# Attention into a gated feed-forward layer on one core: the second batch's keys in three full chunks and a shared half, the weights' high parts on GpSimd, and the second product in groups of units

## The chip, the cores and the metric

The kernel runs on one core of one Trainium2 chip. The metric is the device time of one execution in microseconds (us), median of three runs. The core has a TensorE (PE; its weight loads are shown apart as PEld), a VectorE (DVE), a ScalarE (ACT), a GpSimd (POOL) and a SyncE (SP), which issues most of the DMA transfers.

## The reference

```python
# q, k, v: (4, 12, 448, 64); cap = 30
scores = cap * tanh((q @ k.T / sqrt(64)) / cap)
attn = exp(scores - max) / (sum + 1e-9)
x = (attn @ v)  reshaped to (1792, 768)
out = (sigmoid(x @ w_gate) * (x @ w_val)) @ w_out      # 768 -> 1536 -> 768
```

## The kernel before

The 12 heads of each of the 4 batches are taken two at a time: 24 pairs of heads, numbered n = 0 to 23, six for each batch. A pair holds 448 queries and 448 keys. Its steps are the transposes of keys and queries (`emit_T`), the scores with keys on the partitions (`emit_S`, one chunk of keys m at a time, tanh on ACT), the exponentials (`emit_exp`, ACT), the product with the values (`emit_PV`; the values carry 64 columns of ones, so that the sums of the exponentials come out beside it), the reciprocal of the sums and the scaling (`emit_rd`, `emit_out`). The row x of a batch, split into a high and a low fp32r part (`xspl`), then goes through the feed-forward layer, `moe(b)`. Every large product is made of three fp32r products: high by low, high by high, low by high.

`moe(b)` eats 36 units of weights. The first 24 are columns of w_gate and w_val in turn (a unit is 18 matmuls on tile `h`); the other 12 are pieces of w_out for the product on the tiles `o`: two halves t of 384 columns, each with six units of `KU` = 2 chunks of the inner dimension, and for each unit six matmuls for each of three chunks of rows (five in the last batch). One `o` tile is kept for each chunk of rows during a half, and a half's units come one after the other.

In batch 0 each unit is made from 64-bit input: `convert_w` has one ACT step (L739) and three DVE steps (L740 to L742), and `split_w` makes the high part (`o.hi`, L207 on ACT; on POOL for the first four units) and the low part (`o.lo`, L213 on DVE). Four buffers `wspl` (`WB`) hold split units, and two hold raw ones (`pair`). The split units are stored in device memory, and later batches load them (`load_to`, `wspl<-wd`, 768 KB each) when a buffer comes free. The first four units (`KEEP`) are stored through ACT's queue when PE takes them.

The attention of batch 0 runs by itself at the start. That of batch b + 1 runs between the pieces of `moe(b)`: both are generators, and each `yield` tells how much PE work was emitted; the loop at the kernel's end takes from the one that is behind its share. `o.head` is the attention's expected amount for a head. PE and ACT run in the order in which the code is written; the order on DVE, POOL and SP is a scheduler's.

Three kinds of pairs exist. Pairs 0 to 5 (`alone`) and 6 to 11 multiply exponentials and values in plain fp32 (`direct`); the others split the exponentials. Pairs 0 to 5 are `packed`: three chunks of 128 keys, and the last 64 keys of both heads side by side in one chunk, whose scores are three matmuls over all 128 rows and whose values (`emit_R`) are two matmuls of 64 rows, one for each head. Pairs 6 to 11 are `even`: four chunks of 112 keys for each head. Tiles in PSUM come from `two_banks` (two buffers of two banks), `ps_v` (one bank) and `ps_m` (three banks, for `h`, `o` and some `pv`).

Of the kernel before, what the change touches and what calls it, by code (L numbers as in the profile page):

```python
# [9 lines left out]
F32 = mybir.dt.float32  # L10
# [9 lines left out]
P = 128  # L20
# [78 lines left out]
def _load_inside(engines, t, src, n, runs=False):  # L99

    s = _pair(src, n)
    order = "(p c) d -> p c d" if runs else "(c p) d -> p c d"
    for h in range(2):
        engines[h % len(engines)].dma_start(
            out=t[0:src.shape[2] // NCH, :, h, :], in_=s[h].rearrange(order, c=NCH)
        )


def _load_evenly(nc, t, src, n):

    s = _pair(src, n)
    for h in range(2):
        nc.sync.dma_start(
            out=t[0:src.shape[2] // NCH, h * NCH:(h + 1) * NCH],
            in_=s[h].rearrange("(p c) d -> p c d", c=NCH),
        )
# [63 lines left out]
class _Ops:  # L180
# [37 lines left out]
    def load_qk(self, n, evenly=False, packed=False):  # L218
# [4 lines left out]
        if packed:  # L223
            _load_k_packed(self.nc, [self.nc.sync], qk[:, 1], self.k, n)
        elif evenly:
            _load_inside([self.nc.sync], qk[:, 1], self.k, n, runs=True)
        else:
            _load_k(self.nc, qk[:, 1], self.k, n)
# [20 lines left out]
def _bounded_attention(o, x_done):  # L249
# [32 lines left out]
    packed = alone  # L282
# [5 lines left out]
    def even(n):  # L288

        return direct(n) and not packed(n)  # L290

# [4 lines left out]
    o.head = lambda b: 25 if direct(b * o.NPAIR) else 17.8 if b == B - 1 else 18.5  # L296
# [19 lines left out]
    def load_v(n):  # L316
# [8 lines left out]
        if packed(n):  # L325
            _load_v_packed(nc, s[:, :, 0:D], o.v, n)
        else:
            _load_evenly(nc, s[:, :, 0:D], o.v, n)
# [11 lines left out]
    def emit_T(n):  # L340
# [5 lines left out]
        if even(n):  # L346
            o.transpose_evenly(ps[:, 0, :], t[:, 1])
        else:
            for m in range(NC):
                nc.tensor.transpose(  # L350
                    ps[:, 0, m * P:(m + 1) * P], t[:, 1, m].rearrange("p h d -> p (h d)"), ident
                )
        o.transpose_evenly(ps[:, 1, :], t[:, 0])
        T[n] = ap.tile([P, 2, 2, BANK], F32R, tag="T", bufs=1, name=f"T{n}")
        w = S if even(n) else BANK
        hi, lo = T[n][:, 0, :, 0:w], T[n][:, 1, :, 0:w]
        if even(n):
            parts = [(hi, lo, ps[:, :, 0:w])]
        else:
            parts = [tuple(  # L360
                x.rearrange("p i s -> p (i s)")[:, 0:BANK + S] for x in (hi, lo, ps)
            )]
        for a, b, x in parts:
            o.hi("a", a, x)
            with o.tc.high_priority(offset=2 * AHEAD_OF):
                o.lo("v", b, x, a)

    def emit_S(n, m):
# [3 lines left out]
        w = QC if even(n) else P  # L372
        kh, kl = (T[n][:, i, 0, m * w:(m + 1) * w] for i in range(2))
# [3 lines left out]
        if packed(n) and m == NF:  # L377
            for i, (a, r) in enumerate(ops):
                nc.tensor.matmul(
                    ps[:, 0, 0:S], a, r, start=(i == 0), stop=(i == len(ops) - 1)  # L380
                )
            nc.scalar.activation(
                Pt[n][:, 0, NF, :], ps[:, 0, 0:S], AF.Tanh, scale=c["scale"]
            )
            return 4
        for i, (a, r) in enumerate(ops):
            for j in range(2):
                rows = half(j)
                nc.tensor.matmul(  # L389
                    ps[0:w, j, 0:S], a[rows], r[rows], start=(i == 0), stop=(i == len(ops) - 1)  # L390
                )
        nc.scalar.activation(  # L392
            Pt[n][0:w, :, m, :], ps[0:w, :, 0:S], AF.Tanh, scale=c["scale"][0:w]
        )
        return 4

    def emit_exp(n, j):
        rows = slice(0, QC if even(n) else P)
        t = Pt[n][rows, j, 0:NF if packed(n) and j == 1 else NC]
        nc.scalar.activation(t, t, AF.Exp, scale=c["cap"][rows])  # L400
# [20 lines left out]

    def new_pv(n, j):
        if alone(n) and not (j == 1 and n % 2 == 0):
# [14 lines left out]
    def emit_PV(n, j):  # L438
# [9 lines left out]
        if direct(n):  # L448
            for m in range(NC):
                nc.tensor.matmul(  # L450
                    pv, vs[n][0:QC, j * NC + m, :], Pt[n][0:QC, j, m, :], start=(m == 0),
                    stop=(m == NC - 1),
                )
                if m % 2 == 1:
                    yield 7.4
        else:
            (ph, pl), v = Phl.pop((n, j)), vs[n][:, j]
            for m in range(NF):
                nc.tensor.matmul(pv, v[:, m, :], pl[:, m, :], start=(m == 0), stop=False)  # L459
                nc.tensor.matmul(pv, v[:, m, :], ph[:, m, :], start=False, stop=False)  # L460
            nc.tensor.matmul(pv, v[:, NF, :], ph[:, NF, :], start=False, stop=True)  # L461
            yield 7
# [55 lines left out]
    qks[1] = o.load_qk(1, direct(1), packed(1))  # L518
    load_v(0)
    qks[2] = o.load_qk(2, direct(2), packed(2))  # L520
# [5 lines left out]
    for n in range(NP + 1):  # L526
        live, last = n < NP, n == o.NPAIR
        if live:
            due = emit_S(n, 0) + emit_S(n, 1)
            if n in PLAN:  # L530
# [519 lines left out]
```

## Time and profile before

| | |
|---|---|
| median of 3 runs | 758.19 us (757.61 to 758.44) |
| profiled execution | 757.79 us, its span 756.0 us |
| PE busy in the span | 742.5 us |
| DVE, ACT, POOL busy | 503.5, 379.4, 215.8 us |
| mean granted TensorE clock | 0.998 of full speed |

The span runs from the first to the last instruction; the rest of the time lies around it. PE's busy time counts overlapping matmuls once, so a matmul's own duration is longer than the step from one to the next. Stages in the span: batch 0's attention to about 75 us, batch 0's `h` units to 208.7, its `o` units to 264.8, and the same for the batches after it.

### The profile page before, as it was taken

The numbers are of one execution on the slowest core, as the hardware profiler recorded it, in microseconds if no ns is written. First come the engines' busy times: TensorE is split into PE (matmuls) and PEld (weight loads), VectorE is DVE, ScalarE is ACT, GpSimd is POOL, SyncE is SP. The second block draws the span as 40 slices with busy tenths as digits, with TensorE's granted clock in tenths as the row PEclk, the third lists the DMA queues.
The fourth block names the chain that finished last, engine by engine and source line by source line (L and its number), as shares of the span: only waits on it lengthen the run. The fifth ranks groups of instructions, "written<-read, shape, count | busy, mean of one in ns | idle before, by whom it ended". The sixth has DMA issues, their size and how long they took to land.

```text
span 756.0 us, 10362 instructions
## 1 busy us (share of the span) xinstructions
PE 742.5 (98%) x3922; PEld 642.4 (85%) x3922; DVE 503.5 (67%) x539; ACT 379.4 (50%) x419; POOL 215.8 (29%) x223
## 2 busy tenths in 40 slices
PE   8999999999999999999999999999999999999997
PEld 7555878788788888888899988888989999999996
DVE  2698788978989948988896638899877132322000
ACT  5888567767667456756574146655651011111000
POOL 1354010021210516464555305455452000000000
PEclk9999999999999999999999999999999999999999
DMA  4767898988899864444567954533369945463551
GB/s 100 214 160 164 277 335 262 302 283 263 257 268 379 264 250 127 136 152 139 165 175 241 307 165 134 145 107 123 126 176 328 321 155 182 154 195 98 180 164 57
DMA packets 133511, 151.78 MB, mean 201 GB/s; under 512 B 86860, under 2 KB 111948, under 8 KB 133452
## 3 DMA queue, kind: packets, MB, share of 16 engines
q1 hardware_dynamic: 131788, 147.56, 62.9%
q10 hardware_dynamic: 1664, 3.46, 1.3%
q8 instruction: 33, 0.54, 0.3%
q14 instruction: 26, 0.21, 0.1%
HBM read 118.75 MB, written 31.46 MB: 199 GB/s over the span
## 4 chain that ended last, share of the span: by engine, by line
PE 85%; DVE 6%; DMA 3%; ACT 2%; POOL 2%; issue 1%; SPq 0%; POOLq 0%; DVEq 0%; ACTq 0%
PE h L863 43%; PE o L954 22%; PE sc L389 6%; PE pv L450 4%; DMA wd<-wspl 2%; PE pv L460 2%; PE pv L459 2%; DVE rd L506 2%; PE tp L242 1%; PE pv L441 1%; PE tp L350 1%; DVE pair L742 1%; PE pv L461 1%; DMA v<-in_v_dram 1%; PE dn L498 1%
## 5 line engine op out<-in xcount | busy, mean ns | idle before, releaser
L863 PE MATMUL h<-xspl,wspl 128*128 128x448 f32 x1728 | 377.2, 372 | 0.1
L863 PEld LDWEIGHTS h<-xspl,wspl 128*128 128x128 f32 x1728 | 321.3, 188 | 41.9 <-issue 14.8
L954 PE MATMUL o<-wspl,gspl 128*128 128x384 f32 x864 | 159.5, 338 | 1.2 <-DVE gate L907 1.2
L954 PEld LDWEIGHTS o<-wspl,gspl 128*128 128x128 f32 x864 | 150.4, 188 | 6.0 <-issue 3.8
L205 POOL TENSOR_SCALAR gspl<-gate 128x448 fp32r<-128x448 f32 x48 | 41.3, 860 | 239.4 <-DVE gate L907 239.4
L392 ACT ACTIVATE t<-sc,scale 128x896 f32<-128x896 f32 (+1 forms) x90 | 85.9, 1003 | 33.1 <-PE sc L389 32.8
L207 ACT ACTIVATE wspl<-pair 128x768 fp32r<-128x768 f32 x68 | 57.4, 845 | 88.8 <-PE h L863 75.1
L907 DVE SCALAR_TENSOR_TENSOR gate<-gate,h 128x448 f32<-128x448 f32 x48 | 29.6, 616 | 83.6 <-PE h L863 69.1
L400 ACT ACTIVATE t<-t,capv 128x1792 f32<-128x1792 f32 (+2 forms) x48 | 83.2, 1738 | 0.1
L213 DVE TENSOR_TENSOR wspl<-pair,wspl 128x768 fp32r<-128x768 f32 x68 | 75.3, 1108 | 4.0 <-ACT wspl L207 3.9
L506 DVE RECIPROCAL rd<-rd 128x448 f32<-128x448 f32 x24 | 70.7, 2946 | 5.8 <-ACT rd L479 3.1
L904 ACT ACTIVATE gate<-h 128x448 f32<-128x448 f32 x48 | 26.0, 542 | 92.4 <-PE h L863 87.9
L389 PE MATMUL sc<-T 64*128 64x448 f32 (+1 forms) x540 | 69.1, 383 | 1.9 <-DVE T L213 1.7
L389 PEld LDWEIGHTS sc<-T 64*128 64x128 f32 (+1 forms) x540 | 46.4, 181 | 22.4 <-issue 11.2
L412 POOL TENSOR_TENSOR a<-t 128x448 f32<-128x448 f32 x24 | 31.4, 1309 | 76.6 <-ACT t L400 42.6
L976 DVE TENSOR_SCALAR osb<-o 128x384 f32<-128x384 f32 x22 | 11.9, 556 | 61.9 <-PE o L954 61.8
L207 ACT ACTIVATE ph<-t 128x1792 fp32r<-128x1792 f32 x24 | 40.7, 1698 | 14.8 <-PE pv L461 14.7
L213 DVE TENSOR_TENSOR pl<-t,ph 128x1344 fp32r<-128x1344 f32 x24 | 47.2, 1967 | 0.4
L213 DVE TENSOR_TENSOR gspl<-gate,gspl 128x448 fp32r<-128x448 f32 x48 | 38.1, 794 | 7.2 <-POOL gspl L205 6.9
L213 DVE TENSOR_TENSOR T<-tp,T 128x960 fp32r<-128x960 f32 (+1 forms) x24 | 27.3, 1135 | 22.8 <-ACT T L207 22.7
L742 DVE SCALAR_TENSOR_TENSOR pair<-w,pair 128x768 uint16<-128x768 uint32 x36 | 41.8, 1164 | 0.3
L739 ACT ACTIVATE pair<-w 128x768 f32<-128x768 f32 x36 | 32.5, 905 | 17.4 <-DVE wspl L213 12.3
(81 smaller groups left out, 735.0 us busy)
## 6 DMA issues: line engine op xcount, KB each, us to landing
wspl<-wd SPq DMA_DIRECT2D x72, 768.0 KB, 5.0
wd<-wspl SPq DMA_DIRECT2D x20, 768.0 KB, 5.5
pair<-wr SPq DMA_DIRECT2D x36, 384.0 KB, 3.1
w<-in_moe_w_gate_dram SPq DMA_DIRECT2D x12, 768.0 KB, 6.9
w<-in_moe_w_val_dram SPq DMA_DIRECT2D x12, 768.0 KB, 6.5
w<-in_moe_w_out_dram SPq DMA_DIRECT2D x12, 768.0 KB, 6.5
qk<-in_q_dram SPq DMA_DIRECT2D x46, 112.0 KB, 3.3
wr<-pair SPq DMA_DIRECT2D x12, 384.0 KB, 5.4
```

Of the source, the lines that this page charges most:

```text
L205: self.nc.gpsimd.tensor_scalar(dst, src, 1.0, 1.0, ALU.mult, ALU.mult)
L207: self.nc.scalar.activation(dst, src, AF.Copy)
L213: e.tensor_sub(dst, src, hi.bitcast(F32))
L389: nc.tensor.matmul(ps[0:w, j, 0:S], a[rows], r[rows], start=(i == 0), stop=(i == len(ops) - 1))
L392: nc.scalar.activation(Pt[n][0:w, :, m, :], ps[0:w, :, 0:S], AF.Tanh, scale=c["scale"][0:w])
L400: nc.scalar.activation(t, t, AF.Exp, scale=c["cap"][rows])
L412: nc.gpsimd.tensor_add(a, t[:, 0, :], t[:, 1, :])
L506: nc.vector.reciprocal(rd, rd)
L739: nc.scalar.activation(x, top.bitcast(F32), AF.Copy, scale=2.0 ** -112)
L742: nc.vector.scalar_tensor_tensor(half, low.bitcast(U32), 2.0 ** -29, half, ALU.mult, ALU.add)
L863: nc.tensor.matmul(ps, a, r, start=(kk == 0 and i == 0), stop=(kk == KD - 1 and i == 2))
L954: nc.tensor.matmul(ps, a, r, start=(y + kk == 0 and i == 0), stop=(y + kk == KF - 1 and i == 2),)
```

## The change

Pairs 6 to 11 become `packed` too. For them (`together`) the loop has a branch of its own, in which the values of both heads are multiplied in one run, into two banks of one `two_banks` tile, and the last chunk's scores go to `ps_v`. All 36 units of batch 0 have their high part made by POOL. In the second product the first two units of a half, and the last two, are taken as a group: all their matmuls for a chunk of rows before the next chunk. Units 0 to 2 are stored during the last pairs of batch 0 instead of when PE takes them. `o.head` for batch 1 goes from 25 to 23.5.

```diff
-    packed = alone
+    packed = direct
+    def together(n):
+        return direct(n) and not alone(n)
...
-    o.head = lambda b: 25 if direct(b * o.NPAIR) else 17.8 if b == B - 1 else 18.5
+    o.head = lambda b: 23.5 if direct(b * o.NPAIR) else 17.8 if b == B - 1 else 18.5
...
+        if packed(n) and m == NF:
+            if together(n) and n > o.NPAIR:
+                ps = o.ps_v.tile([P, S], F32, tag="v", name=f"sc{n}_{m}")
+            else:
+                ps = o.two_banks(f"sc{n}_{m}")[:, 0, 0:S]
...
     def new_pv(n, j):
-        if alone(n) and not (j == 1 and n % 2 == 0):
+        if together(n):
+            if j == 0:
+                two[n] = o.two_banks(f"pv{n}")
+            pv = two[n][:, j, 0:S] if j == 0 else two.pop(n)[:, j, 0:S]
+        elif alone(n) and not (j == 1 and n % 2 == 0):
...
+        if n > 0 and together(n - 1):
+            emit_R(n - 1)
+            emit_S(n, 0)
+            yield 5
+            for j in range(2):
+                for _ in emit_PV(n - 1, j):
+                    yield 6
+            for j in range(2):
+                emit_rd(n - 1, j)
+            emit_out(n - 1)
+            vs.pop(n - 1)
+            load_v(n + 1)
+            yield 8
+            emit_S(n, 1)
+            emit_S(n, 2)
+            if not packed(n):
+                yield 8
+            emit_S(n, NF)
+            yield 8
+            emit_T(n + 1)
+            qks[n + 2] = o.load_qk(n + 2, packed(n + 2))
+            yield 5
...
+            emit_exp(n, 0)
+            if not direct(n):
+                emit_P(n, 0)
+            emit_exp(n, 1)
+            split_v(n + 1)
...
+            if NC <= n <= o.NPAIR:
+                o.store_early(n - NC)
...
-        o.hi("p" if u < o.early else "a", s[:, 0, :], t)
+        o.hi("p" if u < NU else "a", s[:, 0, :], t)
...
-                for y in range(x, KF if x >= by_chunk else x + KU, KU):
-                    units.append((y, next_w(u)))
+                if x >= by_chunk:
+                    to = KF
+                elif x == 0 or not end and x == KF - 2 * KU:
+                    to = x + 2 * KU
+                else:
+                    to = x + KU
+                for y in range(x, to, KU):
+                    units.append((y, next_w(u) if y == x or end else w_spl.pop(u)))
...
+                if to > x + KU and not end:
+                    prepare_w(u - 1)
```

On PE, in the middle of `moe(0)`'s first product, the values of pair 7 (`pv`) and the first scores of pair 8 (`sc`) stood like this before:

```order
L389 MATMUL sc_0_1071<-T_982 112x448 x6
L389 MATMUL sc_1_1079<-T_982 112x448 x6
L863 MATMUL h_1_3_1048<-xspl_4_655,wspl_902 128x448 x3
L863 MATMUL h_1_3_1048<-xspl_5_697,wspl_902 128x448 x3
L863 MATMUL h_0_4_1106<-xspl_0_319,wspl_955 128x448 x3
L863 MATMUL h_0_4_1106<-xspl_1_405,wspl_955 128x448 x3
L450 MATMUL pv_0_1113<-t_834,vo_829 128x448 x2
L863 MATMUL h_0_4_1106<-xspl_2_491,wspl_955 128x448 x3
L863 MATMUL h_0_4_1106<-xspl_3_573,wspl_955 128x448 x3
L863 MATMUL h_0_4_1106<-xspl_4_655,wspl_955 128x448 x3
L863 MATMUL h_0_4_1106<-xspl_5_697,wspl_955 128x448 x3
L450 MATMUL pv_0_1113<-t_834,vo_829 128x448 x2
```

The same place of the changed kernel, one pair later (values of pair 8, first scores of pair 9):

```order
L413 MATMUL pv_1318<-t_1088,vo_935 128x448 x2
L365 MATMUL sc_0_1322<-T_1245 128x448 x6
L874 MATMUL h_0_6_1305<-xspl_4_667,wspl_1147 128x448 x3
L874 MATMUL h_0_6_1305<-xspl_5_712,wspl_1147 128x448 x3
L874 MATMUL h_1_6_1350<-xspl_0_319,wspl_1193 128x448 x3
L874 MATMUL h_1_6_1350<-xspl_1_405,wspl_1193 128x448 x3
L420 MATMUL pv_1318<-t_1088,vo_935 128x448 x3
L874 MATMUL h_1_6_1350<-xspl_2_491,wspl_1193 128x448 x3
L874 MATMUL h_1_6_1350<-xspl_3_579,wspl_1193 128x448 x3
L874 MATMUL h_1_6_1350<-xspl_4_667,wspl_1193 128x448 x3
L420 MATMUL pv_1318<-t_1088,vo_935 128x448 x3
L874 MATMUL h_1_6_1350<-xspl_5_712,wspl_1193 128x448 x3
```

A pair's values go from four groups of two matmuls to two matmuls of 64 rows and two groups of three, and half of the first scores comes later.

On PE, in `moe(0)`'s second product, the last two units of the first half (`wspl_1911`, `wspl_1963`) and the start of the second half before:

```order
L954 MATMUL o_0_0_1856<-wspl_1911,gspl_733 128x384 x6
L450 MATMUL pv_0_2066<-t_1772,vo_1767 128x448 x2
L954 MATMUL o_0_1_1857<-wspl_1911,gspl_733 128x384 x6
L954 MATMUL o_0_2_1858<-wspl_1911,gspl_733 128x384 x6
L954 MATMUL o_0_0_1856<-wspl_1963,gspl_733 128x384 x6
L450 MATMUL pv_0_2066<-t_1772,vo_1767 128x448 x2
L954 MATMUL o_0_1_1857<-wspl_1963,gspl_733 128x384 x6
L954 MATMUL o_0_2_1858<-wspl_1963,gspl_733 128x384 x6
```

The same two units (`wspl_1971`, `wspl_1982`) in the changed kernel:

```order
L970 MATMUL o_0_0_1877<-wspl_1971,gspl_751 128x384 x6
L970 MATMUL o_0_0_1877<-wspl_1982,gspl_751 128x384 x6
L420 MATMUL pv_2039<-t_1786,vo_1639 128x448 x3
L970 MATMUL o_0_1_1878<-wspl_1971,gspl_751 128x384 x6
L970 MATMUL o_0_1_1878<-wspl_1982,gspl_751 128x384 x6
L420 MATMUL pv_2039<-t_1786,vo_1639 128x448 x3
L970 MATMUL o_0_2_1879<-wspl_1971,gspl_751 128x384 x6
L970 MATMUL o_0_2_1879<-wspl_1982,gspl_751 128x384 x6
```

The second unit of a group is now wanted six matmuls after the first instead of eighteen, and both buffers come free at the group's end.

On POOL, at the same stage, the changed kernel's queue (with the tiles' numbers: `wspl27` is unit 27, `vs12` the split values of pair 12, `xspl1_4` part 4 of batch 1's row):

```order
L195 TENSOR_SCALAR vs12_2001<-v12_1853 128x8x64
L195 TENSOR_SCALAR wspl27_1886<-pair0_66 128x768
L195 TENSOR_SCALAR gspl0_751<-gate0_11_1766 128x448
L195 TENSOR_SCALAR xspl1_4_1872<-xraw1_929 128x448
L195 TENSOR_SCALAR wspl28_1971<-pair0_66 128x768
L195 TENSOR_SCALAR wspl29_1982<-pair0_66 128x768
L195 TENSOR_SCALAR wspl30_2016<-pair0_66 128x768
L195 TENSOR_SCALAR wspl31_2057<-pair0_66 128x768
L195 TENSOR_SCALAR vs13_2344<-v13_2114 128x8x64
L195 TENSOR_SCALAR wspl32_2122<-pair0_66 128x768
L195 TENSOR_SCALAR xspl1_5_2111<-xraw1_929 128x448
L195 TENSOR_SCALAR wspl33_2143<-pair0_66 128x768
```

Before, none of the `wspl` rows stood there; the sums of pair 12's exponentials (`a12`), which follow the last unit now, stood between `xspl1_4` and `vs13`.

## Rows read from the trace of the kernel before

**Rows 1.** The page, part 1: busy us, share of the span, instructions.

```profile
PE 742.5 (98%) x3922; PEld 642.4 (85%) x3922; DVE 503.5 (67%) x539; ACT 379.4 (50%) x419; POOL 215.8 (29%) x223
```

**Rows 2.** Windows: length, busy PE, PEld, DVE, ACT, POOL, clock, DMA share, GB/s.

```profile
75.00:209.00 134.00, 133.27 (x649) 106.19 (x647) 113.76 (x135) 91.07 (x110) 19.00 (x20) 1.00 0.88 281
209.00:265.00 56.00, 54.95 (x305) 47.51 (x304) 51.81 (x58) 35.11 (x39) 14.95 (x11) 1.00 0.91 306
...
556.00:599.00 43.00, 41.78 (x235) 40.75 (x234) 25.07 (x28) 8.61 (x9) 11.06 (x11) 1.00 0.96 297
```

**Rows 3.** The chain that ended last, from 104 us: start, us, what (records).

```profile
118.51 1.50 PE pv L450 x4
120.01 2.45 PE h L863 x12
...
127.01 1.42 PE sc L389 x12
```

**Rows 4.** The same chain, batch 0's attention.

```profile
66.87 0.75 PE pv L434 x4
67.62 4.71 PE pv L441 x12
```

**Rows 5.** Waits from 75 to 265 us: engine, line, waited for, us, times, longest.

```profile
ACT wspl L207 <- DMA wd<-wspl: 4.7, 2, 2.8
```

**Rows 6.** Timeline of PE at batch 2's second product; in brackets the idle time before.

```profile
557.67 2.36 PE L954 MATMUL o<-wspl,gspl 128*128 128x384 f32 x12 [1.22 <-DVE gate L907]
```

**Rows 7.** Timeline of DVE in batch 0's second product.

```profile
205.62 0.93 DVE L740 TENSOR_SCALAR pair<-pair 128x768 int32<-128x768 int32 x1
...
217.26 0.56 DVE L740 TENSOR_SCALAR pair<-pair 128x768 int32<-128x768 int32 x1 [0.98 <-ACT pair L739]
...
218.73 0.95 DVE L213 TENSOR_TENSOR wspl<-pair,wspl 128x768 fp32r<-128x768 f32 x1
...
242.60 0.56 DVE L740 TENSOR_SCALAR pair<-pair 128x768 int32<-128x768 int32 x1 [1.22 <-ACT pair L739]
...
251.06 2.50 DVE L213 TENSOR_TENSOR pl<-t,ph 128x1344 fp32r<-128x1344 f32 x1
...
254.54 1.81 DVE L213 TENSOR_TENSOR wspl<-pair,wspl 128x768 fp32r<-128x768 f32 x1
...
256.88 2.94 DVE L506 RECIPROCAL rd<-rd 128x448 f32<-128x448 f32 x1
...
262.70 1.56 DVE L213 TENSOR_TENSOR xspl<-xraw,xspl 128x448 fp32r<-128x448 f32 x1 [0.46 <-POOL xspl L205]
```

**Rows 8.** Timeline of PE in the same stage.

```profile
208.71 1.21 PE L954 MATMUL o<-wspl,gspl 128*128 128x384 f32 x6
...
250.25 13.02 PE L954 MATMUL o<-wspl,gspl 128*128 128x384 f32 x72
263.20 1.49 PE L389 MATMUL sc<-T 64*128 64x448 f32 x12
```

**Rows 9.** POOL's wspl group by form, then timelines of POOL and DVE around 205 us.

```profile
L205 POOL TENSOR_SCALAR wspl<-pair 128x768 fp32r<-128x768 f32 x4 | 3.3, 832 | 4.0 <-DVE pair L742 4.0
...
204.47 3.38 POOL L205 TENSOR_SCALAR xspl<-xraw 128x448 fp32r<-128x448 f32 x4 [2.79 <-ACT gate L904]
211.68 2.16 POOL L205 TENSOR_SCALAR gspl<-gate 128x448 fp32r<-128x448 f32 x1 [3.83 <-DVE gate L907]
...
206.47 0.96 DVE L213 TENSOR_TENSOR xspl<-xraw,xspl 128x448 fp32r<-128x448 f32 x1
...
208.58 0.61 DVE L213 TENSOR_TENSOR xspl<-xraw,xspl 128x448 fp32r<-128x448 f32 x1
...
212.44 0.98 DVE L741 SCALAR_TENSOR_TENSOR pair<-w,pair 128x768 int32<-128x768 int32 x1
```

**Rows 10.** DMA issues from 556 to 599 us (count, KB, us to landing); PE there.

```profile
wspl<-wd SPq DMA_DIRECT2D x12, 768.0 KB, 6.2
...
581.68 17.02 PE L954 MATMUL o<-wspl,gspl 128*128 128x384 f32 x96
```

More of the change, by code (lines that the diff above doesn't have):

```diff
@@ L96, in _pair, with _load_inside @@
     return src[b, 2 * p:2 * p + 2]
-def _load_inside(engines, t, src, n, runs=False):
+def _load_inside(engines, t, src, n):
     s = _pair(src, n)
-    order = "(p c) d -> p c d" if runs else "(c p) d -> p c d"
     for h in range(2):
         engines[h % len(engines)].dma_start(
[L105 to L115, printed above, removed]
+            out=t[0:src.shape[2] // NCH, :, h, :],
+            in_=s[h].rearrange("(c p) d -> p c d", c=NCH),
         )
@@ L324, in load_v @@
         nc.gpsimd.memset(s[:, :, D:], 1.0)
[L325 to L328, printed above, removed]
+        _load_v_packed(nc, s[:, :, 0:D], o.v, n)
         vs[n] = s
@@ L345, in emit_T @@
         ps = o.two_banks(f"tp{n}")
[L346 to L352, printed above, removed]
+        for m in range(NC):
+            nc.tensor.transpose(
+                ps[:, 0, m * P:(m + 1) * P], t[:, 1, m].rearrange("p h d -> p (h d)"), ident
+            )
         o.transpose_evenly(ps[:, 1, :], t[:, 0])
         T[n] = ap.tile([P, 2, 2, BANK], F32R, tag="T", bufs=1, name=f"T{n}")
[L355 to L366, printed above, removed]
+        a, b, x = (
+            y.rearrange("p i s -> p (i s)")[:, 0:BANK + S]
+            for y in (T[n][:, 0], T[n][:, 1], ps)
+        )
+        o.hi("a", a, x)
+        with o.tc.high_priority(offset=2 * AHEAD_OF):
+            o.lo("v", b, x, a)
     def emit_S(n, m):
@@ L420, in emit_P @@
         Asum[n, j] = s
+    two = {}
     def new_pv(n, j):
[L423 removed]
+        if together(n):
[3 more added lines that the diff above has]
+        elif alone(n) and not (j == 1 and n % 2 == 0):
             pv = o.ps_m.tile([P, S], F32, tag="m", name=f"pv{n}_{j}")
@@ L447, in emit_PV @@
         pv = new_pv(n, j)
[L448 to L462, printed above, removed]
+        (ph, pl), v = Phl.pop((n, j)), vs[n][:, j]
+        for m in range(NF):
+            nc.tensor.matmul(pv, v[:, m, :], pl[:, m, :], start=(m == 0), stop=False)
+            nc.tensor.matmul(pv, v[:, m, :], ph[:, m, :], start=False, stop=False)
+        nc.tensor.matmul(pv, v[:, NF, :], ph[:, NF, :], start=False, stop=True)
+        yield 7
     def row(n):
@@ L584, in _bounded_attention @@
             return
-        emit_exp(n, 1)
+        if not first:
+            emit_exp(n, 1)
         split_v(n + 1)
@@ L850, in next_w, with store_early @@
         load_raw_to(u + LEAD + 2)
-        w = w_spl.pop(u)
-        if u < KEEP:
-            store_w(u, w, nc.scalar)
-        return w
+    def store_early(u):
+        if u < KEEP and u not in w_dram:
+            store_w(u, w_spl[u], nc.scalar)
+    def next_w(u):
+        prepare_w(u)
+        store_early(u)
+        return w_spl.pop(u)
     def moe(b):
```

55 lines of the change are left out of this document (24 added, 31 removed).

## The prediction

> **What bounds the kernel now.** First the page's busy times: PE works 742.5 of the span's 756.0 us [rows 1], so what the change is worth is PE's work and PE's 13.5 idle us, and any other engine counts only where PE comes to wait for it. Second, the windows. The change touches batch 0's feed-forward stage, 75 to 265 us, where the attention of batch 1 runs in between, and the second products of the later batches. From 75 to 209 us PE is busy 133.27 of 134, from 209 to 265 it is 54.95 of 56, and from 556 to 599 it is 41.78 of 43 [rows 2]. The reader should look at DVE in the same rows: 113.76 of 134, then 51.81 of 56. In batch 0's second product DVE is 93% busy, so PE's lead there is short. Third, the chain that ended last: in batch 0's stage it goes through PE piece by piece, and so tells what a piece costs in the stream.
>
> **PE's work.** A pair of batch 1 now multiplies its values in four groups of two fp32 matmuls of 112 rows, 1.50 us a group [rows 3]: 6.0 us, 0.75 for a matmul. Afterwards it is six matmuls of 128 rows and two of 64 rows, one for each head. Batch 0's pairs do just that: the two of 64 rows took 0.75 us together, the price of one, and six full ones 4.71 [rows 4]. In the stream I take 0.75 each, as in rows 3, so 4.5 + 0.75 = 5.25, a gain of 0.75; with 4.71 it is 0.54. The scores go from 24 half-height matmuls at 1.42 for 12 [rows 3] = 2.84, to 18 of them, 2.13, and three of full height at 2.45 / 12 = 0.20 each, together 2.74: 0.1 less. Four transposes get 16 columns wider, which I let cancel this. Six pairs: **-4.5** (bounds -3.2 and -5.1).
>
> **Waits that go.** The stores of units 0 to 2 leave before the stage; today ACT, about to overwrite their buffers, waits twice for them, 4.7 us [rows 5], with the exponentials queued behind. PE's 0.73 idle us from 75 to 209 lie there: **-0.7** (0 to -0.7). In the second product the third `o` tile needs the bank that DVE frees with the last gate step. Today it is wanted 12 matmuls after the product's start, with groups 24 after. In batch 2 PE waited 1.22 us there [rows 6]; I take **-0.9** (0 to -1.2). Batch 0's 1.05 idle us in its second product [rows 2] count as **-1.0** (0 to -1.05).
>
> **What DVE gives back.** 32 high parts (units 4 to 35) go from ACT to POOL. Alone such an operation took 0.83 us [rows 9]. Beside a busy DVE, POOL's operations stretch: a smaller one, on 448 columns, took 2.16 while DVE's step beside it took 0.98, as alone; but with four POOL operations back to back DVE's took 0.96 against 0.61 [rows 9]. So one costs DVE between 0 and 0.35; a full exclusion would be 0.83. I take 0.2, since single operations are like the first row and DVE sometimes waits for the high part itself.
>
> In the first product that is 23 x 0.2 = 4.6 on DVE's 113.8 us, in a stretch that stays near 133 (it loses 3.75 and 0.7 and gets 3.0 of pair 10's values from the next): not the bound, so 0.
>
> In the second product it is. DVE's stretch from the conversion of unit 27 to the low part of unit 35 runs from 205.62 to 254.54 + 1.81 = 256.35 [rows 7], 50.7 us with little idle. By the changed order it loses the split of pair 12's exponentials (2.50) and gets pair 11's reciprocal and last row split (2.94 + 1.56). POOL's sums of pair 12 now come behind the units, so that the last low part, 1.81 today, should take the 0.95 of an undisturbed one. The two waits for ACT's conversion step, 0.98 + 1.22, should go, since ACT loses nine operations there. Nine high parts add 9 x 0.2 = 1.8. Together 50.7 + 2.0 - 0.9 - 2.2 + 1.8 = 51.4. After unit 35's low part come 30 matmuls, at 17.02 / 96 = 0.177 [rows 10] 5.3 us, and 1.49 of scores [rows 8]. The stretch begins 208.71 - 205.62 = 3.1 before the first `o` matmul, so DVE lets the next batch's first product start 51.4 - 3.1 + 6.8 = 55.1 after it. PE's own work there is 54.95 less half of pair 10's values (3.0, now ahead of it) less 0.75 = 51.2. Nothing else covers the difference: today unit 35 is ready at 256.35 and its first matmul runs near 263.2 - 18 x 0.177 = 260.0 [rows 8], and 3.7 us of lead is all there is. DVE gives back **+3.9** (0, if the conversions get further ahead; 9.6, if each high part costs 0.83; 2.2 more if ACT's waits stay). The late things are the low parts of units 29 and 35.
>
> The Trainium skill (GPSIMD Engine Reference, Key points) says that GpSimd shares its SBUF interfaces with VectorE and contends with instructions that have two SBUF inputs or a two-port mode, which DVE's conversions and low parts are; that speaks against the change. The trace agrees that they disturb each other, but mostly at POOL's cost, as told. By the rule taken as a full exclusion the sum would be that of the fifth case below.
>
> **What the groups cost.** With four buffers, both units of a group come free together, and in batches 1 and 2 two loads of 768 KB are issued at once for a group that starts 36 matmuls, 6.4 us, later where no attention lies between. Today a load lands 6.2 us after issue (median), and every unit has 54 matmuls, 9.6 us [rows 10]. So the first just lands in time; a second at the 297 GB/s of this window [rows 2] would come 2.6 us behind it, at 8.8, and is wanted six matmuls (1.1 us) after the first, at 7.5: 1.3 late. There are three such places in each of the two batches (units 4 and 5, 8, 10 and 11); half of them have attention in between. Bounds 0 and, with 1.5 at six places, 9; I take **+0.3**, since batch 1's later half and batch 2's alone are open, and a late load there finds a queue that has just emptied. POOL and SP work in order too: a high part that waits for its buffer holds back `gspl`, `xspl` and the ones-memsets, all wanted a pair later or at the stage's end; on SP, unit 35's store stands before the load of the next batch's second unit, which is wanted 18 matmuls after the first.
>
> Sum: -4.5 - 0.7 - 0.9 - 1.0 + 3.9 + 0.3 = -2.9, and 757.8 - 2.9 = 754.9 for an execution like the profiled one. The median of before is 0.4 above it, so **755.3**.
>
> **The rivals.**
> 1. The forecast, DVE giving back half: 755.3, own range 753 to 757. Chance 0.40.
> 2. The cover holds: DVE never comes last, as for 0 delay beside the single POOL operation in rows 9, and no load is late: -7.1, so 750.7 + 0.4 = 751.1. Against it: DVE's 51.81 of 56 us. 0.20.
> 3. The gain is eaten: 0.35 for each high part (+1.4), and ACT's waits stay (+2.2), because POOL's high part comes later than ACT's did and holds the raw buffer: -2.9 + 3.6 = +0.7, 758.9. For it: POOL's stretched rows. 0.21.
> 4. Slower by loads: each of the six places waits 1.5 us, +8.7 on the forecast, 764. It decides from 0.8 us a place on. Against it: rows 2 show only 0.91 to 0.96 of the DMA engines' time, not a queue that grows. 0.10.
> 5. Slower by exclusion: every high part holds DVE for 0.83. The second product loses 5.7 more; in the first, 113.8 + 19.1 = 132.9 us of DVE meet 132.6 of PE, about 1 more: -2.9 + 6.7 = +3.8, 762.0. 0.09. (The page of the Trainium skill named above would make this of it, if sharing the interfaces meant shutting each other out.)
>
> That the change does not do what it says would be two 64-row matmuls taking 1.5 together; rows 4 show 0.75.
>
> **How the numbers follow.** About 0.2% (1.5 us) is what a measurement of this kernel can tell from no change. Cases 1 and 2 are faster: 0.60. Case 3 is the same: 0.21. Cases 4 and 5 are slower: 0.19. The time is the first case's. The range of 750 to 760 takes in cases 2 and 3 and the bounds of PE's work, and leaves out 4 and 5.
>
> **What would show it.** PE's work: the values of a pair of batch 1 in 5.25 us, in a 0.75 and two 2.25 pieces. The waits: no ACT wait for the stores of the first units, no PE wait for the gate step at a second product's start. DVE: PE idle before `o` matmuls of units 28, 29 or 35, ended by DVE's `wspl`, and batch 0's second product at 55 us rather than 51; high parts on POOL of 1 to 2 us. Groups: no PE wait ended by `wspl<-wd`. The prediction is wrong if PE shows no such wait for DVE (then 751), or if PE waits for loads in batches 1 and 2 or DVE's low parts take 1.5 us throughout (then 758 or more).

## The result, and the profile after

The changed kernel takes **762.94 us** (median of 5 runs, 762.15 to 765.1) against 757.61 for the kernel before in the same rounds: a ratio of **1.0074**, 95% interval 1.0062 to 1.0087. It is slower; the forecast was 755.3 and the range ended at 760. The profiled execution took 762.94 us with a span of 761.1.

The starts of the first matmul of each stage, read off PE's records, say where the time went (us):

| stretch | before | after | difference |
|---|---|---|---|
| start to batch 0's first product | 74.98 | 75.48 | +0.50 |
| batch 0, first product | 133.73 | 131.48 | -2.25 |
| batch 0, second product | 56.08 | 60.77 | **+4.69** |
| batch 1 and batch 2's first product | 289.40 | 289.57 | +0.17 |
| batch 2, second product | 44.35 | 46.19 | **+1.84** |
| batch 3 | 157.47 | 157.55 | +0.08 |

The gain stands in the second row. More than twice of it is lost in the third, and the fifth loses again. The page of the changed kernel, part 1 (busy us, share, instructions), answers to [rows 1]:

```profile
PE 742.9 (98%) x3904; PEld 644.3 (85%) x3904; DVE 510.1 (67%) x539; ACT 351.0 (46%) x387; POOL 240.1 (32%) x267
```

PE is busy as long as before although it has less to do. The windows of [rows 2], now (columns as there):

```profile
75.00:209.00 134.00, 134.00 (x654) 108.50 (x652) 122.56 (x136) 73.20 (x90) 39.95 (x50) 1.00 0.84 271
209.00:265.00 56.00, 50.87 (x270) 44.38 (x269) 50.78 (x56) 24.50 (x26) 17.98 (x17) 0.94 0.81 268
556.00:599.00 43.00, 40.48 (x224) 38.76 (x223) 26.46 (x28) 11.16 (x12) 13.43 (x13) 1.00 0.87 261
```

The first product is full of PE. In the second PE is idle for 5.1 of 56 us, and the granted clock, the last column but two, is 0.94 where it was 1.00. Two shorter windows show that loss apart:

```profile
225.50:228.90 3.40, 3.40 (x13) 2.03 (x12) 2.71 (x4) 1.03 (x1) 1.43 (x2) 0.50 1.03 305
...
259.70:263.00 3.30, 3.30 (x12) 3.30 (x11) 3.29 (x2) 0.00 (x0) 2.92 (x2) 0.50 0.94 256
```

For 3.4 us each the clock is at the lower of its two levels, 1.2 GHz; both stretches begin where PE takes up work again after an idle time. PE's own waits in that stage (waited for, us, times, longest), then one each of ACT, POOL and DVE:

```profile
PE o L970 <- DVE wspl L203: 2.6, 2, 1.8
PE pv L413 <- ACT t L373: 2.6, 1, 2.6
...
ACT pair L745 <- DVE wspl L203: 13.0, 4, 4.3
...
POOL wspl L195 <- PE o L970: 15.1, 5, 5.0
...
DVE wspl L203 <- POOL wspl L195: 3.5, 4, 1.4
```

The chain that ended last (start, us, what) shows how they come about, ahead of it one pair's values in the first product:

```profile
113.62 0.95 PE pv L413 x4
...
117.21 2.25 PE pv L420 x6
...
121.29 2.25 PE pv L420 x6
...
216.46 4.19 PE o L970 x24
...
220.78 0.85 POOL wspl L195
...
221.65 0.97 DVE wspl L203
...
222.65 0.90 ACT pair L745
223.54 1.69 ACT t L373
...
225.27 1.70 PE pv L413 x4
...
227.47 1.39 POOL wspl L195
...
228.88 1.58 DVE wspl L203
...
230.51 1.31 PE o L970 x6
...
256.53 0.85 POOL wspl L195
...
257.40 1.89 DVE wspl L203
...
259.34 7.05 PE o L970 x30
```

Read it as one loop over in-order engines. POOL's high part of unit 28 ends at 221.6, DVE's low part follows and frees a raw buffer, ACT, which has waited 4.30 us for that buffer, makes its conversion step, and only then comes to the exponentials that stand behind it; PE, whose next matmuls want them, has been idle for 2.55 us. Units 29 and 35 then keep PE waiting directly. The 30 matmuls behind unit 35 take 7.05 us where 0.177 each [rows 10] would be 5.3.

What POOL's high parts wait for is DVE, not one of the four `wspl` buffers. The view of waits puts 15.1 us of them down to PE, which frees those buffers, and so the chain comes to POOL from PE's 24 matmuls. But the view names the semaphore that moved last before the instruction, and POOL's records of its waits in the trace tell them apart. For unit 28 the wait on DVE ends at 220.29, 0.05 us after that unit's third conversion step, and those on PE and on a DMA are over by 220.38. For unit 35 the times are 256.34, 0.05 us after the step, and 256.43. From unit 27 to unit 35 every wait on DVE ends within 0.1 us of the unit's third step; in unit 32 alone another one follows, of 0.6 us. The two steps, and unit 35's low part beside POOL's first sum of pair 12's exponentials (timelines):

```profile
219.19 1.04 DVE L748 SCALAR_TENSOR_TENSOR pair<-w,pair 128x768 uint16<-128x768 uint32 x1
...
255.22 1.07 DVE L748 SCALAR_TENSOR_TENSOR pair<-w,pair 128x768 uint16<-128x768 uint32 x1
...
257.40 1.88 DVE L203 TENSOR_TENSOR wspl<-pair,wspl 128x768 fp32r<-128x768 f32 x1
```
```profile
257.33 1.14 POOL L385 TENSOR_TENSOR a<-t 128x448 f32<-128x448 f32 x1
```

In batch 2's second half the chain of the same kernel has become one of loads (below it, PE's wait for them):

```profile
581.19 6.92 DMA wspl<-wd
...
588.15 3.73 PE o L970 x20
591.88 6.26 DMA wspl<-wd
...
598.18 5.47 PE o L970 x30
```
```profile
PE o L970 <- DMA wspl<-wd: 2.5, 3, 1.6
```

### The profile page after: what moved, and what is told of

It is laid out like the page before. It is cut to its first block, busy times and chain, and to the rows that moved or that the text cites. A ratio compares the mean times of both kernels' runs of the same rounds, so it can differ in the third digit from the quotient of the medians.

```text
span 761.1 us, 10418 instructions
## 1 busy us (share of the span) xinstructions
PE 742.9 (98%) x3904; PEld 644.3 (85%) x3904; DVE 510.1 (67%) x539; ACT 351.0 (46%) x387; POOL 240.1 (32%) x267
## 4 chain that ended last, share of the span: by engine, by line
PE 91%; DMA 4%; DVE 2%; POOL 1%; SPq 1%; ACT 1%; issue 1%; ACTq 0%; POOLq 0%
PE h L874 47%; PE o L970 22%; PE sc L365 7%; PE pv L420 5%; PE pv L430 2%; PE pv L429 2%; DMA wspl<-wd 2%; PE tp L332 1%; PE pv L413 1%; DMA qk<-in_k_dram 1%; PE tp L230 1%; DMA qk<-in_q_dram 1%; PE sc L358 1%; PE pv L431 1%; PE dn L468 1%; DVE wspl L203 1%
## 5 line engine op out<-in xcount | busy, mean ns | idle before, releaser
L874 PE MATMUL h<-xspl,wspl 128*128 128x448 f32 x1728 | 372.9, 370 | 0.0
L368 ACT ACTIVATE t<-sc,scale 128x896 f32<-128x896 f32 x84 | 80.8, 1005 | 43.0 <-PE sc L365 42.7
L195 POOL TENSOR_SCALAR gspl<-gate 128x448 fp32r<-128x448 f32 x48 | 37.9, 789 | 166.7 <-DVE gate L918 166.7
L373 ACT ACTIVATE t<-t,capv 128x1792 f32<-128x1792 f32 (+1 forms) x48 | 80.4, 1690 | 0.0
L365 PE MATMUL sc<-T 64*128 64x448 f32 x504 | 68.4, 395 | 2.3 <-DVE T L203 2.2
L365 PEld LDWEIGHTS sc<-T 64*128 64x128 f32 x504 | 44.7, 186 | 22.9 <-issue 14.0
L197 ACT ACTIVATE wspl<-pair 128x768 fp32r<-128x768 f32 x36 | 30.4, 845 | 69.1 <-PE h L874 65.8
L195 POOL TENSOR_SCALAR wspl<-pair 128x768 fp32r<-128x768 f32 x36 | 33.8, 941 | 89.4 <-DVE pair L748 33.8
L420 PE MATMUL pv<-t,vo 128*128 128x448 f32 x144 | 58.6, 544 | 0.0
L420 PEld LDWEIGHTS pv<-t,vo 128*128 128x128 f32 x144 | 26.4, 189 | 22.4 <-issue 22.1
```

What stands on the lines that cost most here:

```text
L195: self.nc.gpsimd.tensor_scalar(dst, src, 1.0, 1.0, ALU.mult, ALU.mult)
L197: self.nc.scalar.activation(dst, src, AF.Copy)
L365: nc.tensor.matmul(ps[:, j, 0:S], a[rows], r[rows], start=(i == 0), stop=(i == len(ops) - 1))
L368: nc.scalar.activation(Pt[n][:, :, m, :], ps[:, :, 0:S], AF.Tanh, scale=c["scale"])
L373: nc.scalar.activation(t, t, AF.Exp, scale=c["cap"])
L420: nc.tensor.matmul(pvs[n, j], vs[n][:, j * NC + m, :], Pt[n][:, j, m, :], start=False, stop=(m == NF - 1),)
```

## The experiments

Their texts say VectorE, GpSimd and ScalarE for DVE, POOL and ACT. At the start the suspects were the high parts on POOL (theory A), the groups (B), and that the packed pairs bring nothing by themselves (C); A2, that DVE's work bounds batch 0's second product, came up with the first results, and E asks whether the high parts on POOL cost time in the kernel before. Medians in us, with the ratio to the kernel before and its interval; then the lengths of batch 0's first and second product and of batch 2's second product in the profiled execution, and how long the granted clock was at 0.5 in batch 0's second product. The code of batch 0 is the same in the changed kernel and e11, and in e9 and e10; in both pairs the second products differ by 1.4 us, with one more stretch at the low clock in the longer one. Batch 2's second product lies between 45.05 and 46.24 in the six runs that have the changed kernel's groups there (after, e1, e5, e6, e9, e15). Differences of that size between two rows say little.

| run | median | ratio, interval | first | second | batch 2 | clock low |
|---|---|---|---|---|---|---|
| before | 757.61 | | 133.73 | 56.08 | 44.35 | 0 |
| after | 762.94 | 1.0074 (1.0062-1.0087) | 131.48 | 60.77 | 46.19 | 6.8 |
| e1 | 762.59 | 1.0064 (1.0046-1.0082) | 132.77 | 58.59 | 45.47 | 3.4 |
| e2 | 765.60 | 1.0089 (1.0064-1.0115) | 131.48 | 65.46 | 44.47 | 13.7 |
| e3 | 759.06 | 1.0020 (1.0009-1.0031) | 132.78 | 57.68 | 44.23 | 0 |
| e4 | 759.55 | 1.0019 (1.0009-1.0028) | 131.48 | 60.16 | 44.12 | 3.4 |
| e5 | 753.90 | 0.9947 (0.9931-0.9964) | 131.48 | 51.86 | 45.91 | 0 |
| e6 | 760.90 | 1.0037 (1.0023-1.0051) | 131.48 | 60.68 | 45.05 | 6.8 |
| e7 | 757.97 | 0.9997 (0.9988-1.0007) | 132.76 | 56.32 | 44.85 | 0 |
| e8 | 758.28 | 1.0004 (0.9994-1.0014) | 132.51 | 57.95 | 44.76 | 0 |
| e9 | 770.25 | 1.0170 (1.0157-1.0184) | 131.48 | 67.19 | 45.69 | 10.2 |
| e10 | 766.23 | 1.0109 (1.0094-1.0123) | 131.48 | 68.55 | 42.79 | 13.7 |
| e11 | 759.82 | 1.0025 (1.0014-1.0036) | 131.48 | 59.36 | 43.87 | 3.4 |
| e12 | 762.63 | 1.0064 (1.0051-1.0077) | 133.75 | 60.47 | 44.15 | 3.4 |
| e13 | 751.07 | 0.9911 (0.9895-0.9926) | 131.48 | 51.86 | 43.90 | 0 |
| e14 | 757.29 | 0.9992 (0.9983-1.0001) | 132.78 | 56.42 | 43.71 | 0 |
| e15 | 764.02 | 1.0079 (1.0066-1.0093) | 132.58 | 62.19 | 46.24 | 6.8 |
| e16 | 761.21 | 1.0043 (1.0030-1.0057) | 132.58 | 61.74 | 42.81 | 6.8 |
| e17 | 756.70 | 0.9990 (0.9981-0.9999) | 132.84 | 55.72 | 43.03 | 0 |
| e18 | 760.98 | 1.0042 (1.0028-1.0056) | 132.57 | 61.67 | 42.79 | 6.8 |

**e1: the high parts of units 4 to 35 back on ACT.**
```diff
-        o.hi("p" if u < NU else "a", s[:, 0, :], t)
+        o.hi("p" if u < o.early else "a", s[:, 0, :], t)
```


> The changed kernel with the high parts of units 4 to 35 back on ACT, the rest as changed. Theory A (the high parts on POOL come late and slow DVE, so that PE waits for exponentials and low parts in batch 0's second product): the 5.1 us of PE waits there and the 3.4 us at the lower clock behind them go, the time falls from 762.9 to 754 to 756. Theory B (the groups ask for two units at once, whoever makes the high part): PE still waits there, 760 to 763. Both leave the loads' waits in batch 2's second product, about 2.5 us.


A miss for theory A: the median hardly moves and lies in theory B's range. The second product is 2.2 us shorter, of which one stretch less at the low clock makes some 1.7, and the first 1.3 longer; PE's idle time in the second is the same, 5.1 us. In it DVE is busy for only 46.42 of 56 us, and PE waits all the same. DVE waits too, for ACT's conversion step now (windows, then waits):

```profile
209.00:265.00 56.00, 50.91 (x282) 45.36 (x280) 46.42 (x54) 32.41 (x36) 8.32 (x7) 0.97 0.81 272
```
```profile
PE pv L413 <- issue: 3.0, 1, 3.0
PE sc L365 <- ACT t L368: 2.1, 1, 2.1
...
DVE pair L746 <- ACT pair L745: 5.8, 3, 2.5
```

**e2: no groups.**
```diff
-                elif x == 0 or not end and x == KF - 2 * KU:
-                    to = x + 2 * KU
```


> The changed kernel with every unit of the second product by itself, as before; high parts on POOL. Theory A: batch 0's second product still waits for DVE, only the loads' waits of batch 2 go (-2.5) and the wait for the gate step comes back (+1.2): 760 to 762. Theory B: the waits of both batches go, 753 to 755.


No theory gave this. Batch 2's loss goes, but batch 0's second product takes 65.46 us: PE now waits 2.9 us for DVE's gate step and 4.5 for its output copies, which stand behind conversions and a reciprocal in DVE's order.

**e3: both edits of e1 and e2**, so that the packed pairs and the early stores remain.

> The changed kernel with neither: high parts on ACT and every unit by itself, so that the packed pairs, their one run of values and the early stores are left. Both theories: PE's work of 4.5 us less is all seen, with 1.2 us of the gate wait in batch 2: 752.5 to 754.5. If the packed pairs or their order in the stream are at fault themselves (theory C): over 757.


759.06: the pairs do not pay by themselves. What the first product gains, the second loses.

**e4: only the first two units of a half grouped.**
```diff
-                elif x == 0 or not end and x == KF - 2 * KU:
+                elif x == 0:
```


> The changed kernel with the first two units of a half grouped, the last two not; high parts on POOL. Theory A: batch 0 hardly changes (1 us less, since unit 29 is wanted later), the loads' waits of batch 2 shrink to under 1 us: 759 to 761. Theory B: about half of the waits of batch 0 stays, 756 to 759.


3.4 us of the loss go, 2.1 of them in batch 2: the last group is the one that costs there.

**e5: DVE's third conversion step left out for units 24 to 35.** This leaves the low bits of those units' weights out of the computation; it takes 12 steps of 1.05 us from DVE.
```diff
-        nc.vector.scalar_tensor_tensor(
-            half, low.bitcast(U32), 2.0 ** -29, half, ALU.mult, ALU.add
-        )
+        if u < 24:
+            nc.vector.scalar_tensor_tensor(
+                half, low.bitcast(U32), 2.0 ** -29, half, ALU.mult, ALU.add
+            )
```


> The changed kernel without DVE's third conversion step (the low bits of the 64-bit input) for units 24 to 35: twelve DVE steps of 1.05 us, 12.6 us, left out around batch 0's second product. Theory A2 (DVE's queue is the bound of that stage; what PE saves there, PE waits): the waits for exponentials and low parts and the low clock behind them go, 754 to 756. Theory D (DVE's queue stands still there for loads or POOL, and its work is not what binds): under 2 us less, over 761.


This one decides the place: the second product falls by 8.9 us to 51.86, without a wait of PE and without a fall of the clock. Here is the same window as for e1, its last 6.2 us already batch 1's; the third busy time, behind PE's and PEld's, is DVE's, 43.33 of 56 us:

```profile
209.00:265.00 56.00, 56.00 (x318) 49.76 (x318) 43.33 (x50) 27.10 (x29) 20.97 (x20) 1.00 0.95 325
```

The step left out is the one that POOL's high parts were seen to wait for. It shortens each unit's chain as well as DVE's work, so this run does not tell the two apart.

**e6: batch 0's six output tiles copied out by ACT**, 3.3 us less for DVE; **e7: the same on e3.**
```diff
-                elif m % 2 == 0 or b < B - 1:
+                elif b > 0 and (m % 2 == 0 or b < B - 1):
```


> The changed kernel with batch 0's six finished o tiles copied out by ACT instead of DVE, 6 x 0.56 us off DVE. Theory A2: 2 to 4 us less, 759 to 761. Theory D: no change, 762 to 763.

> The kernel with high parts on ACT and single units (759.1 before) and batch 0's o tiles copied out by ACT. There PE waited 2.6 us for DVE's copies of o tiles, which stood on DVE behind the split values of pair 13, and those behind their load. Theory D: these 2.6 us go, 756 to 757. Theory A2: the gain is the 3.4 us of DVE's work, 755.5 to 757; the two differ in what PE waits for next: loads (D) or low parts (A2).


Both are faster than what they start from, by 2.0 and 1.1 us; e7 is level with the kernel before, and above both of its ranges. In e6 the profiled stage is no shorter, so its gain is not shown to come from there.

**e8: the kernel before, with the high parts of all units on POOL.**

> The kernel before with the high parts of all 36 units on POOL and nothing else changed. Theory A2: with PE's old work DVE's lead at the second product's end was 3.7 us, nine high parts cost DVE about 0.35 each, so nearly nothing is lost: 757 to 759. If POOL's queue itself is late (theory E: it works in order, and split values or rows that wait for others hold the high parts back): PE waits for low parts, 760 to 764.


The move alone costs nothing that can be measured. In the profiled execution the second product is 1.9 us longer and the first 1.2 shorter, and no wait of PE there is for a low part. What the move costs DVE does show, since the instructions are the same as before: 513.4 us busy against 503.5 [rows 1], on average 0.31 us for each of 32 high parts.

```profile
PE 743.3 (98%) x3922; PEld 643.3 (85%) x3922; DVE 513.4 (68%) x539; ACT 355.0 (47%) x387; POOL 248.7 (33%) x255
```

**e9: after, with the low parts of units 28 to 35 on POOL; e12: the same on the kernel before.**
```diff
-        o.lo("p" if u < o.early else "v", s[:, 1, :], t, s[:, 0, :])
+        o.lo("p" if u < o.early or 28 <= u < NU else "v", s[:, 1, :], t, s[:, 0, :])
```


> The changed kernel with the low parts of units 28 to 35 made by GpSimd instead of VectorE; nothing is left out of the computation. The eight low parts of VectorE are about 1.1 us each, 9 us of the 51 us that it is busy from 209 to 265 us; GpSimd is busy there for 18 us, and one low part takes it 1.83 us (the one at the start of batch 0). Theory A2 (VectorE's work is the bound in batch 0's second product): that stage falls from 60.8 us to 53 to 55, the granted clock stays at 1.0 in it, and the time is 755 to 757. Rival F (GpSimd's two-operand subtractions hold VectorE's other instructions up by about as much as they take off it): the stage stays within 1.5 us of 60.8 and the time is 761 to 764, with the mean of VectorE's conversion steps above 1.2 us where it was 1.04. Rival G (a chain of conversion, high part and low part of 0.9 + 1.8 us on GpSimd is late for TensorE): TensorE waits for GpSimd's low parts, time 758 to 761.

> The kernel before with the low parts of units 28 to 35 made by GpSimd and nothing else. Its second product of batch 0 takes 56.1 us. Theory A2: in the kernel before VectorE bounds that stage too (it is busy 58.3 of 61 us there in the variant with the high parts on GpSimd), so this alone gives 1.5 to 3 us: 755 to 756.5. Rival: before is bound there by TensorE and its order, and this changes less than 0.8 us. By rival F it is slower, 759 or more.


An attempt to relieve DVE that does the opposite: 7.3 and 4.5 us worse, and e9 is above every range given for it. Rival F is shown in e12 by the timelines of POOL and DVE (start, us, line, operation):

```profile
225.79 2.13 POOL L213 TENSOR_TENSOR wspl<-pair,wspl 128x768 fp32r<-128x768 f32 x1 [0.58 <-ACT wspl L207]
...
239.59 2.50 POOL L213 TENSOR_TENSOR wspl<-pair,wspl 128x768 fp32r<-128x768 f32 x1 [4.12 <-PE sc L389]
244.03 2.00 POOL L213 TENSOR_TENSOR wspl<-pair,wspl 128x768 fp32r<-128x768 f32 x1 [1.94 <-ACT wspl L207]
```
```profile
226.14 2.60 DVE L741 SCALAR_TENSOR_TENSOR pair<-w,pair 128x768 int32<-128x768 int32 x1
...
236.46 0.96 DVE L741 SCALAR_TENSOR_TENSOR pair<-w,pair 128x768 int32<-128x768 int32 x1
...
239.46 0.96 DVE L741 SCALAR_TENSOR_TENSOR pair<-w,pair 128x768 int32<-128x768 int32 x1
...
244.37 2.47 DVE L741 SCALAR_TENSOR_TENSOR pair<-w,pair 128x768 int32<-128x768 int32 x1
```

The same step takes 0.96 us with POOL at rest (236.46) and 2.60 and 2.47 beside a two-operand step of POOL that began before it. Both end 0.8 us after POOL's step does, nearly their whole length alone, so they got almost nothing done beside it. The step at 239.46 began 0.13 us before POOL's; it took its 0.96, and POOL's, at 2.50, was the longest of the three. In e9 a part of rival G comes on top: PE waits 7.8 us for two of POOL's low parts.

**e10 and e11: the last group in batch 0 alone**, on e9 and on the changed kernel.
```diff
-                elif x == 0 or not end and x == KF - 2 * KU:
+                elif x == 0 or b == 0 and x == KF - 2 * KU:
```


> The same as the run before it, and the last two units of a half are taken together in batch 0 alone, so that batches 1 and 2 load those two one after the other as in the kernel before; nothing is left out of the computation. In batch 2 the stretch from the second half's start to the next batch was 22.5 us in the changed kernel and 19.35 before. If the loads asked for together are late there, this gives back 2 to 3 us against the run before it: 752.5 to 754.5 by theory A2. If the loads are late because of the first two units' group (which stays), it gives back under 1 us.

> The changed kernel with the last two units of a half taken together in batch 0 alone; nothing else is changed. Theory: the last group's two loads cost 2 to 3 us in batch 2, batch 0's second product stays at 60.8 us: 760 to 761. Rival: the loads are late anyway, within 0.7 us of the changed kernel's 762.9. The run that kept only the first groups had 20.5 us for the stretch in question, against 22.5, so about 2 us is the middle.


The loads' part came out: batch 2's second product is 2.3 us shorter in e11 (2.9 in e10), and the medians fall by 3.1 and 4.0. The absolute time of e10 is a miss, since it hung on A2 for e9.

**e13: e5, with groups in batches 1 and 2 at the start of a first half alone.** It leaves out what e5 leaves out.
```diff
-                elif x == 0 or not end and x == KF - 2 * KU:
+                elif x == 0 and (b == 0 or t == 0) or b == 0 and x == KF - 2 * KU:
```


> The run without VectorE's third conversion step for units 24 to 35 (it leaves out the low bits of those units' weights), and in batches 1 and 2 the only groups left are those at the start of a first half. Theory A2 with the loads as the second cost: batch 0 as in that run (210 to 184 us from its start to batch 1's), batch 2's second product 43 to 43.3 us where that run took 45.9 and the kernel before 44.4, and the time is 751 to 752, which is about what the sum would be if VectorE gave nothing back. Rival: the loads of batch 2 are late for another reason, time 753.3 to 754.5.


As expected, 751.07, though batch 2's second product took 43.90 us where 43 to 43.3 was expected. PE is busy without a gap through both of batch 0's products:

```profile
75.00:209.00 134.00, 134.00 (x653) 108.50 (x652) 120.26 (x134) 73.17 (x90) 39.88 (x51) 1.00 0.83 273
209.00:265.00 56.00, 56.00 (x319) 49.67 (x318) 43.39 (x50) 27.09 (x29) 20.86 (x20) 1.00 0.93 319
```

**e14: e7, with groups only at the start of the first half of batches 1 and 2.**
```diff
+                elif x == 0 and t == 0 and b > 0:
+                    to = x + 2 * KU
```


> The changed kernel with the high parts on ScalarE, batch 0's output tiles copied out by ScalarE, and groups only at the start of the first half of batches 1 and 2; nothing is left out. The same without those groups took 757.97. If the groups' gain is the wait for the gate step alone (1.2 us in batch 2, none in batch 1 where attention lies between), the time is 756.4 to 757; if the grouped loads eat it, 757.6 to 758.5.


757.29, between the two: the gate step's wait is gone (batch 2's second product -1.1 us against e7), and a load still keeps PE waiting for 0.6.

**e15 to e18: three raw buffers instead of two**, on the changed kernel, on it with e13's groups, on e14, and on e16 with e6's copies.
```diff
-    WRAW = 2
+    WRAW = 3
...
-    c["pair0"] = const.tile([P, 3 * n0], F32, name="pair0")
+    c["pair0"] = const.tile([P, 2304], F32, name="pair0")
...
-        v = self.ap.tile([P, 2, NCH, self.D], F32, tag="v", bufs=2, name=f"v{n}")
+        v = self.ap.tile([P, 2, NCH, self.D], F32, tag="v", bufs=1, name=f"v{n}")
```


> The changed kernel with three raw buffers for the weights' conversion instead of two; the space comes from the natural values of batches 2 and 3, which have one buffer instead of two. Nothing is left out. Theory L (the conversion loop through two raw buffers bounds batch 0's second product: ScalarE's step waits 13.0 us there for VectorE's low part, which frees the buffer, and the exponentials stand behind it): the stage falls from 60.8 us to 52 to 56, PE's wait for the exponentials goes, and the time is 754.5 to 759. Theory A2 (VectorE's amount of work bounds it): the order on VectorE changes little, the stage stays at 59 to 61 and the time at 761 to 764.

> The run before it with the groups of batches 1 and 2 only at the start of a first half. Theory L: 2 to 3 us below that run, 752 to 756.5; theory A2: 758 to 761.

> The version with high parts and output copies on ScalarE and groups only in batches 1 and 2 (757.29 with two raw buffers), with three raw buffers. PE's waits there, 1.7 us for an output copy, 1.4 for the gate step and 0.8, are not of the conversion loop: by theory L and A2 both 756 to 757.5.

> The second of these runs with batch 0's six output tiles copied out by ScalarE instead of VectorE. Theory A2: 3.3 us less work for VectorE gives 1 to 2 us, 757 to 759.5. Theory L: VectorE is no bound any more, and a copy behind ScalarE's exponentials can only be later: within 1 us of the second run, 752 to 757.


Theory L falls with e15, at 764.02 and 62.19 us for the stage, which is over theory A2's range as well. ACT's wait for the raw buffer is gone from that stage; ACT waits for the 64-bit loads instead, and PE for DVE's low parts (waits of ACT, then of PE):

```profile
ACT pair L745 <- DMA w<-in_moe_w_out_dram: 8.3, 2, 5.1
...
PE o L970 <- DVE wspl L203: 6.6, 2, 4.9
```

As in the changed kernel, conversions of a later unit stand ahead of the low part that PE wants next: in the chain DVE does two of each of its three steps between 224 and 229 us, and unit 29's low part ends at 231.2 (230.5 in the changed kernel). e18 has 3.3 us less for DVE and is 0.2 us from e16, so these 3.3 us do not decide there; the times of e16 and e18 lie above all ranges given for them. e17, 756.70, is the fastest version that computes everything: 0.9990 of the kernel before (0.9981 to 0.9999), within what counts as no change.

## Why the prediction was wrong

**The step that failed** is the term under "What DVE gives back", "DVE gives back **+3.9**". The place was right and the price too small: with e13 beside the changed kernel, the second product of batch 0 loses 60.77 - 51.86 = 8.9 us. Of these, 5.1 are PE's idle time and some 3.4 the two stretches at the low clock (half of 6.8).

The terms of that working show where. DVE's stretch from unit 27's conversion to unit 35's low part, forecast at 51.4 us, ran from 205.00 to 259.28, 54.3 us. Its work was not the error: DVE was busy for 49.2 us, and the working comes to 50.1 (47.2 before, + 2.0 - 0.9 + 1.8). Its idle time was, 3.6 us before, 1.4 by the working and 5.0 measured. The two waits for ACT's conversion step did go, as "since ACT loses nine operations there" says; in their place DVE waits 3.5 us for POOL's high parts, which come right behind its own third steps. Nor did the last low part fall to 0.95: POOL's first sum began 0.07 us ahead of it, and it took 1.88. Further, PE came to the second product 1.7 us earlier than before and DVE to its stretch 0.6, so DVE's lead was 206.97 - 205.00 = 1.97 us instead of 3.1, although DVE's own delay in the first product had been put at 0. And the matmuls and scores at the end took 8.5 us instead of 6.8, at the low clock, which was in no term. The stretch, the lead and the end, 2.9 + 1.1 + 1.7, make the 5.7 us from the forecast 55.1 to 60.77.

ACT's wait for a raw buffer, which comes free a POOL step and a DVE step later than the conversion, went from 4.7 to 13.0 us, and PE's exponentials stood behind it: the 2.55 us at 225.

**PE's work and the waits at the start: right.** Six pairs, the stores' waits and the idle time of the second product were to give -4.5 - 0.7 - 1.0 = -6.2 in batch 0. In e13, where nothing is late, the two products take 183.34 us against 189.81, -6.5; the estimate of 51.2 us for PE alone in the second met 51.9. The pieces of a pair's values are 2.25, 2.25 and 0.95 in the chain, the last with a score beside it, against 2.25, 2.25 and 0.75 forecast; no wait of ACT for the stores is left.

**The gate step: right,** for batch 2: its first half fell from 25.01 to 23.69 us, 1.3 for a forecast 0.9.

**The loads: mis-sized.** +0.3 was taken because "a late load there finds a queue that has just emptied"; batch 2's second half went from 19.35 to 22.50 us, +3.15, with 2.5 us of waits for loads. The working had set the second load 1.3 us late at six places; in fact batch 1, where attention lies between, lost nothing, and most came at the last group of batch 2 (e11 gives 2.2 of it back). The first load there took 6.92 us, and the next one 6.26 from 591.88, when the matmuls ahead of it had ended.

**The sum again,** in the profiled executions: forecast -2.9, measured 5.05. DVE's term is off by 8.9 - 3.9 = 5.0, the loads by 2.85, the gate step by -0.4, PE and its waits by -0.3; the remaining 0.8 is the start (+0.5, which varied from 74.1 to 76.4 us over all runs) and parts that the change leaves alone.

**The rivals.** The time is near that of the fifth, 762.0, by luck and not by its mechanism. On average a high part on POOL holds DVE for 0.31 us (e8), near the 0.2 taken and far from 0.83, and taking all of them back (e1) leaves the time as it is. The third rival named ACT's wait for the raw buffer, which did grow; but e15 takes it away and gains nothing. The fourth had the loads, at six places, and they were late in batch 2 alone. The second rival's 751.1 is near what e13 measures, where steps are left out to make the cover hold.

**What stays open.** Taking steps out of DVE removes the loss; DVE's busy share does not measure it, since in their own stages e1 has 48.98 of 58.59 us and e5 44.18 of 51.86, 84 and 85%, and only one of them waits. Nor was it the raw buffers alone (e15), the high parts alone (e1) or the groups alone (e2). Another number of `wspl` buffers was not tried; the records of POOL's waits speak against it. Shown is that the chain of a unit's steps over three in-order engines, with attention's steps between them, was late; which position in which queue sets its pace was not tried apart. No version with all of DVE's conversions ended that stage under 55.7 us (e17). Whether that is a floor set by DVE is not shown, as PE's waits in e17 are for ACT's output copies and DVE's gate step.

## What to carry over

In a stage where two engines are both over 90% busy, as PE and DVE were here, ask what the second does when the first gets shorter: with less work for PE, the chain that feeds it showed, and the waits came several at a time, not one at the end. An engine's work can be forecast well and its idle time still be wrong. Follow a late step to everything that stands behind it in each in-order engine, not only to the engine that consumes it, and ask which buffer it frees. Where the profile names a releaser for an instruction with several waits, compare its end with the ends of the others. Units taken together ask for their loads together; it cost nothing where other work lay between, and 2 us where none did.

## What the runs showed that was not expected

- **What POOL does decides what DVE loses.** POOL's one-operand high part cost DVE 0.31 us on average (e8); its two-operand low part made DVE's two-operand step 2.60 and 2.47 instead of 0.96 (e12), when it was the first to begin. The Trainium skill (GPSIMD Engine Reference, Key points) speaks of contention with DVE instructions that have two SBUF inputs; the trace agrees for the second case, and in the first, with the same instructions on DVE, shows a fraction of it on average. A single low part can lose more: in the changed kernel unit 29's took 1.58 us beside the high part of unit 30, where 0.95 is its length alone.
- **A wait of PE cost more than its length.** After waits of 2.55 and 1.81 us PE's granted clock was at 0.5 (1.2 GHz) for 3.4 us each. The length of a wait alone does not tell: in that stage no fall followed one of 1.8 us in e11, of 2.8 in e4 and of 3.0 in e1, and one did follow a wait of 2.1 in e1.
